# Another order of all operations for pooled attention with a SoLU layer on one core

## The chip, the cores and the metric

The kernel runs on one core of a Trainium2 chip. Time is the device time of one execution in microseconds (us); of each kernel the median of several executions is given. The engines are named as in the profile: PE is TensorE (matmuls; PEld its weight loads), DVE is VectorE, ACT is ScalarE, POOL is GpSimd, SP is SyncE, from whose queue every transfer and DMA transpose is issued.

## The reference

Attention over 8 batches and 8 heads with 576 queries and head size 64. Keys and values are averaged over 8 neighbouring rows, so 72 of each are left. The result, 4608 tokens of 512 features, goes through a layer of 1024 hidden features with SoLU (h times its own softmax), a layer norm and a second matrix:

```python
k_p = k.reshape(B, H, Sp, pool, D).mean(axis=3)
v_p = v.reshape(B, H, Sp, pool, D).mean(axis=3)
scores = scale * np.matmul(q, k_p.transpose(0, 1, 3, 2))
attn = np.exp(scores - np.max(scores, axis=-1, keepdims=True))
attn = attn / (np.sum(attn, axis=-1, keepdims=True) + 1e-09)
x = np.matmul(attn, v_p)            # then (B, S, H * D) -> (B * S, 512)
h = x @ w_in
e = np.exp(h - np.max(h, axis=-1, keepdims=True))
solu = h * (e / (np.sum(e, axis=-1, keepdims=True) + 1e-09))
mu = np.mean(solu, axis=-1, keepdims=True)
var = np.mean((solu - mu) ** 2, axis=-1, keepdims=True)
out = ((solu - mu) / np.sqrt(var + 1e-06) * g_ln) @ w_out
```

## The kernel before

The 4608 tokens are 36 tiles of 128. A group of 9 tiles serves two batches: four tiles of the even batch, one tile with the last 64 queries of both (tiles 4, 13, 22, 31), four of the odd batch. Every matrix product is made in float16 with a high and a low part of each operand, so the scale of each operand must be known first.

**Weights** (w_in is wi, w_out is wo; four quarters each, in 64 bits on the way in). Each quarter goes through w_load (SP), w_exp and w_sgn (ACT), w_shift and w_tail (DVE), w_bnd (PE), w_mul (POOL). When all four are there, w_rmax and w_all (DVE) and w_par (PE) give one scale (wi_scale, wo_scale). Then w_hi (ACT) writes the high part; the low part comes from w_res (PE) and w_lo (ACT), for two quarters of w_out from w_lod (DVE).

**Each batch.** load_kv brings k and v in three pieces (kr, vr), load_q brings q. The rows are pooled into kp and vp: by pool_kv on POOL, for batch 0 by pool_pe on PE and pool_ev on ACT, which copies the sums. a_max, a_par, a_all and a_unit give the scale of k and of v, q_max and q_scale that of q. k_hi, k_lo and k_T make k; v_hi, v_lo, v_x, r_hi, r_lo, v_rep and r_put make v (vb).

**Each tile.** In this order:
- q_hi (ACT), q_lo (DVE), q_T (a DMA transpose), scores (PE, 32 matmuls into sc);
- the softmax: s_max, s_sub (DVE), s_exp (ACT), e_sum, e_rec, e_mul (DVE), e_hi (ACT), e_lo (POOL), e_T (a DMA transpose);
- av (PE, 24 matmuls into xp), x_hi (ACT), x_lo (DVE);
- mm1, in three parts of 16 matmuls into hp; the last part needs x_lo (for tiles 0 and 1 the second);
- h_max and h_nb (DVE), h_exp (ACT), three z_scale and z_mul (DVE), z_cen and z_hi (ACT), two z_lo (POOL), z_var (ACT), two z_T (DMA transposes), n_u and n_f (POOL);
- mm2, in three parts of 16 matmuls into op, o_evac (ACT), o_store (SP).

Two buffers hold hp (pool ps_h), in turn: mm1 of a tile can start when z_mul of the tile two places earlier has read its buffer. There is one buffer each for sc (ps_s), xp (ps_x) and op (ps_o). Seven buffers (raw) hold what is loaded of k, v and the weights.

**What sets the order.** There are 2083 operations. Each takes its place from the table ORDER: for each name the places of its first, second, ... use. At the end all are issued in the order of their places; each engine works its own queue strictly in this order, and SP's queue too:

```python
def op(eng, dur, t, fn, *args, r=(), w=(), u=(), after=()):
    name = fn.__name__ + ("." + args[0] if args and isinstance(args[0], str) else "")
    count[name] = count.get(name, -1) + 1
    ops.append((ORDER[name][count[name]], fn, args))
```

```python
with tc.manual_schedule():
    for _, fn, args in sorted(ops, key=lambda o: o[0]):
        fn(*args)
```

The numbers dur, t, r, w, u and after are left from the search of an order and have no effect here. Waits between engines follow from the buffers that the operations read and write.

Of the kernel before, what the change touches and what calls it, by code (L numbers as in the profile page):

```python
# [25 lines left out]
        "a_all.v": (130, 252, 484, 790, 1026, 1176, 1480, 1803),
        "a_max.k": (34, 179, 434, 620, 864, 1120, 1352, 1596),
        "a_max.v": (128, 235, 481, 771, 1001, 1170, 1442, 1770),
        "a_par.k": (35, 182, 448, 651, 877, 1125, 1377, 1613),
        "a_par.v": (129, 236, 483, 786, 1025, 1171, 1479, 1802),  # L30
        "a_unit.k": (39, 57, 211, 213, 451, 455, 657, 663, 882, 890, 1129, 1155, 1390, 1437, 1615,
        1616),
# [5 lines left out]
        "e_T": (221, 239, 275, 332, 402, 425, 572, 497, 628, 712, 641, 761, 825, 873, 933, 957,
        1078, 1145, 1146, 1248, 1263, 1356, 1406, 1476, 1495, 1557, 1647, 1634, 1718, 1748, 1851,
        1887, 1908, 1996, 1942),  # L40
        "e_Tc": (181,),
        "e_Tp": (180,),
        "e_hi": (107, 108, 218, 219, 237, 222, 273, 272, 329, 330, 399, 373, 423, 422, 509, 508,
# [4 lines left out]
        "e_lo": (109, 220, 238, 274, 331, 401, 424, 571, 496, 604, 711, 640, 760, 824, 861, 932,  # L48
        956, 1064, 1144, 1139, 1222, 1261, 1339, 1405, 1475, 1436, 1529, 1633, 1603, 1691, 1746,
        1795, 1886, 1891, 1988, 1933),  # L50
        "e_mul": (97, 147, 195, 269, 317, 372, 415, 505, 452, 556, 689, 622, 753, 785, 820, 892,
        930, 1039, 1109, 1053, 1203, 1242, 1297, 1350, 1430, 1387, 1521, 1586, 1570, 1663, 1713,
        1791, 1834, 1867, 1958, 1924),
# [1496 lines left out]
```

## Time and profile before

| what | value |
|---|---|
| time, median of 3 runs (lowest, highest) | 487.48 us (487.16, 487.89) |
| span of the profiled execution, first to last instruction | 483.6 us |
| what lies around the span, by the median | 3.9 us |
| PE busy | 456.5 us, 94% |
| DVE busy | 372.2 us, 77% |
| ACT busy | 335.2 us, 69% |
| POOL busy | 304.5 us, 63% |

No time of the profiled execution itself was taken; the median of the runs is set beside its span. A share is a mean over the whole span; how it is spread over the opening, the middle and the end is read from the stretches. A wait is counted where an engine stands idle, and put down to what ended it.

### The profile page before, as it was taken

The page shows a single profiled execution, that of the slowest core. Times are in us where ns is not written, and L with a number is a line of the kernel's source. Part 1 is how long each engine was busy: PE and PEld are TensorE (multiplying, and loading weights), DVE is VectorE, ACT ScalarE, POOL GpSimd, SP SyncE. Part 2 cuts the span into 40 slices and gives each one's busy share as a digit, 9 for nine tenths or more (in the row PEclk, how much of TensorE's full clock was granted, in tenths as well). Part 3 has the DMA queues.
Part 4 walks back from the last instruction along what each step waited for, and adds up shares of the span by engine and source line. Part 5 has one row for each costly group of instructions (what it writes and reads, how often), then busy time and mean ns, then how long its engine had stood idle before and what let it go on. Part 6 is the DMA issues. An engine that isn't in the chain of part 4 may idle for free.

```text
span 483.6 us, 14740 instructions
## 1 busy us (share of the span) xinstructions
PE 456.5 (94%) x5976; PEld 287.7 (59%) x5976; DVE 372.2 (77%) x787; ACT 335.2 (69%) x557; POOL 304.5 (63%) x525
## 2 busy tenths in 40 slices
PE   1779899999999999999999999999999999999996
PEld 1655455655655556555556667666776666755553
DVE  5988999999889789878798867678878887462320
ACT  5598887677966688796677657587585697456361
POOL 3459737696697985858953597717758625643532
PEclk9989999999999999999999999999999999999999
DMA  8999389998999899999994999689899576861742
GB/s 309 395 354 225 86 114 219 196 193 138 213 237 213 209 173 207 204 229 229 161 215 111 215 245 172 126 136 243 167 229 190 115 137 117 138 142 24 153 108 69
DMA packets 197749, 88.92 MB, mean 184 GB/s; under 512 B 174121, under 2 KB 182321, under 8 KB 197169
## 3 DMA queue, kind: packets, MB, share of 16 engines
q1 hardware_dynamic: 197680, 87.98, 85.9%
q8 instruction: 47, 0.77, 0.6%
q14 instruction: 22, 0.17, 0.1%
HBM read 36.70 MB, written 9.44 MB: 95 GB/s over the span
## 4 chain that ended last, share of the span: by engine, by line
PE 78%; DVE 16%; DMA 2%; issue 2%; ACT 1%; SPq 0%; POOL 0%; ACTq 0%; DVEq 0%
PE op L274 35%; PE hp L274 31%; PE xp L999 4%; PE sc L274 3%; DMA kr<-in_k_dram 2%; DVE q L866 2%; DVE m L1041 1%; PE krps L410 1%; DVE sc L934 1%; DVE mx L920 1%; DVE sc L923 1%; DVE z L1073 1%; DVE e L949 1%; PE vrps L410 1%; PE res_wi L810 1%
## 5 line engine op out<-in xcount | busy, mean ns | idle before, releaser
L274 PE MATMUL hp<-wi,xT 128*64 128x512 f16 x1728 | 197.2, 379 | 2.8 <-DVE z L1073 1.4
L274 PE MATMUL op<-wo,zT 128*64 128x512 f16 x1728 | 197.2, 379 | 0.1
L274 PEld LDWEIGHTS <-xT 128*64 128x64 f16 x1728 | 106.6, 110 | 75.2 <-ACT xT L1008 2.0
L274 PEld LDWEIGHTS <-zT 128*64 128x64 f16 x1728 | 106.5, 110 | 70.6 <-DMA zT<-z 0.5
L1093 POOL TENSOR_TENSOR z<-z,z 128x512 f16<-128x512 f32 x71 | 82.0, 1167 | 67.9 <-ACT z L1087 66.4
L978 POOL TENSOR_TENSOR e<-e,e 128x512 f16<-128x512 f32 x36 | 42.2, 1173 | 39.7 <-ACT e L972 39.6
L1041 DVE TENSOR_REDUCE m<-hp 128x1 f32<-128x1024 f32 x36 | 43.8, 1217 | 23.1 <-PE hp L274 22.9
L1082 ACT ACTIVATE z<-z,sz 128x1024 f32<-128x1024 f32 x36 | 41.2, 1143 | 17.4 <-DVE z L1073 17.4
L1073 DVE SCALAR_TENSOR_TENSOR z<-hp,rs,z 128x1024 f32<-128x1024 f32 x36 | 46.1, 1280 | 9.1 <-ACT z L1052 7.9
L1052 ACT ACTIVATE z<-hp,nb,Hb 128x1024 f32<-128x1024 f32 x32 | 38.3, 1196 | 11.7 <-DVE nb L1044 9.1
L1151 ACT ACTIVATE osb<-op,f 128x512 f32<-128x512 f32 x36 | 24.5, 679 | 31.3 <-PE op L274 8.1
L1087 ACT ACTIVATE z<-z 128x1024 f16<-128x1024 f32 x36 | 37.7, 1050 | 0.9 <-DMA zT<-z 0.4
L1106 ACT ACTIVATE junk<-z 128x1024 f16<-128x1024 f32 x36 | 37.7, 1048 | 0.3
L400 POOL TENSOR_TENSOR vr<-vr 128x512 f32<-128x512 f32 (+3 forms) x42 | 36.9, 888 | 0.6
L400 POOL TENSOR_TENSOR kr<-kr 128x512 f32<-128x512 f32 (+3 forms) x42 | 36.7, 882 | 1.0 <-DMA kr<-in_k_dram 0.2
L920 DVE TENSOR_REDUCE mx<-sc 128x8 f32<-128x576 f32 x36 | 27.0, 750 | 12.9 <-PE sc L274 12.6
L934 DVE TENSOR_REDUCE sc<-sc 128x8 f32<-128x576 f32 x36 | 27.3, 759 | 12.2 <-ACT sc L930 12.1
L999 PEld LDWEIGHTS <-vb 128*64 128x64 f16 x960 | 28.9, 111 | 6.7 <-DVE vb L574 1.0
L1012 DVE SCALAR_TENSOR_TENSOR xT<-xp,xT 128x512 f16<-128x512 f32 x36 | 24.5, 681 | 8.9 <-ACT xT L1008 8.8
L999 PE MATMUL xp<-eT,vb 128*64 128x128 f16 (+1 forms) x960 | 31.0, 215 | 0.3 <-ACT e L975 0.3
L274 PEld LDWEIGHTS <-qT 128*64 128x64 f16 x1152 | 24.7, 114 | 9.9 <-ACT dg_wi L803 3.4
L1008 ACT ACTIVATE xT<-xp 128x512 f16<-128x512 f32 x36 | 21.2, 589 | 12.2 <-PE xp L999 12.2
(237 smaller groups left out, 621.3 us busy)
## 6 DMA issues: line engine op xcount, KB each, us to landing
kr<-in_k_dram SPq DMA_DIRECT2D x16, 512.0 KB
qr<-in_q_dram SPq DMA_DIRECT2D x16, 512.0 KB
vr<-in_v_dram SPq DMA_DIRECT2D x16, 512.0 KB
out_dram<-osb SPq DMA_DIRECT2D x32, 256.0 KB
wor<-in_moe_w_out_dram SPq DMA_DIRECT2D x4, 1024.0 KB
wo<-in_moe_w_in_dram SPq DMA_DIRECT2D x2, 1024.0 KB
wir<-in_moe_w_in_dram SPq DMA_DIRECT2D x2, 1024.0 KB
zT<-z SPq DMA_TRANSPOSE x72
```

What stands on the lines that cost most here:

```text
L274: nc.tensor.matmul(out[lo : lo + 64] if m > 64 else out, lhsT=lhsT[:, lo : lo + 64], **kw)
L400: nc.gpsimd.tensor_tensor(out=dst, in0=src[:, :, :n], in1=src[:, :, n : 2 * n], op=ALU.add)
L934: nc.vector.tensor_reduce(out=tl[i]["r0"], in_=s_view(i), axis=AX.X, op=ALU.add)
L978: nc.gpsimd.tensor_tensor(out=e_main(i, 1), in0=e_src(i)[0], in1=e_main(i, 0), op=ALU.subtract)
L999: nc.tensor.matmul(xp[64 * e : 64 * e + 64, c, lo:hi], lhsT=vb[b % 2][:, n, c, e], rhs=eT[:, 2 * c + e if n < 2 else H + e, lo:hi], start= ...
L1041: nc.vector.tensor_reduce(out=small(i, "m"), in_=tl[i]["hp"], axis=AX.XY, op=ALU.max)
L1052: nc.scalar.activation(z, t["hp"], AF.Exp, bias=t["nb"], scale=hsc(i, 0), accum_out=small(i, "se"))
L1073: nc.vector.scalar_tensor_tensor(out=t["z"], in0=t["hp"], scalar=t["rs"], in1=t["z"], op0=ALU.mult, op1=ALU.mult, accum_out=small(i, "sz"),)
L1082: nc.scalar.activation(t["zf"], t["zf"], AF.Identity, bias=t["sz"], scale=-float(DFF))
L1087: nc.scalar.activation(t["z16"][:, 0], t["zf"], AF.Copy)
L1093: eng.tensor_tensor(out=t["z16"][:, 1, fs], in0=t["zf"][:, fs], in1=t["z16"][:, 0, fs], op=ALU.subtract)
L1106: nc.scalar.activation(junk, t["zf"], AF.Square, scale=DFF**-0.5, accum_out=small(i, "V"))
```

## The change

The table ORDER holds other numbers; the code below it is the same, five lines further down, since the table has become five lines longer. All 2083 operations remain, with the same operands and buffers. 1395 of the 2083 places hold another operation than before, the last of them place 1856. Two lines of the table as an example:

```diff
-        "a_all.k": (36, 188, 449, 652, 881, 1126, 1380, 1614),
+    "a_all.k": (69, 188, 504, 686, 930, 1130, 1377, 1614),
```

The transfers at the start, in the order of SP's queue: before, w_in 0 and 1, k 2, w_in 2, k 1, k 0, q 0, q 1, w_in 3, w_out 0, g, w_out 1 and 2, v 2, v 1, w_out 3, v 0. Now, w_in 0, g, k 2, v 2, w_in 1 and 2, q 0, k 1, q 1, w_in 3, k 0, w_out 0 and 1, v 1, w_out 2, v 0, w_out 3 (the number is that of the quarter or piece).

PE's order of the tiles in mm1 begins 0, 1, 2, 3, 4, 5, 6, 7, 8, 9, 11, 10 before, and 0, 1, 2, 3, 4, 5, 6, 8, 7, 9, 11, 10 now.

ACT at the start, from the second quarter of w_in on. sg and u are what w_sgn and w_exp write, q_0 is q16 of tile 0, kp_0 the pooled k of batch 0 out of krps. Before:

```order
L675 ACTIVATE sg_wi1_153<-wo_86 128x1024
L634 ACTIVATE u_wi1_155<-wo_86 128x1024
L634 ACTIVATE u_wi2_171<-wir2_169 128x1024
L675 ACTIVATE sg_wi2_174<-wir2_169 128x1024
L421 ACTIVATE kp_0_87<-krps0_160 128x128
L421 ACTIVATE kp_0_87<-krps0_160 64x64
L421 ACTIVATE kp_0_87<-krps0_160 128x128
L862 ACTIVATE q16_0_218<-qr0_182,sq('b', 0)_206 128x8x64
```

Now:

```order
L639 ACTIVATE u_wi1_177<-wo_86 128x1024
L639 ACTIVATE u_wi2_179<-wir2_155 128x1024
L680 ACTIVATE sg_wi1_182<-wo_86 128x1024
L680 ACTIVATE sg_wi2_188<-wir2_155 128x1024
L867 ACTIVATE q16_0_198<-qr0_167,sq('b', 0)_194 128x8x64
L639 ACTIVATE u_wi3_205<-wir3_171 128x1024
L867 ACTIVATE q16_3_254<-qr0_167,sq('b', 0)_194 128x8x64
L867 ACTIVATE q16_1_266<-qr0_167,sq('b', 0)_194 128x8x64
L897 ACTIVATE qT0_268<-qTp0_245 128x1024
L680 ACTIVATE sg_wi3_273<-wir3_171 128x1024
L426 ACTIVATE kp_0_87<-krps0_212 128x128 x2
L426 ACTIVATE kp_0_87<-krps0_212 64x64
```

The copies into kp_0 (pool_ev) stood ahead of q_hi of tile 0 and of w_exp of the last quarter; now they stand behind three q_hi, that w_exp, the copy of qT0 and a w_sgn.

DVE ahead of z_mul of tile 4, the last row. The number in a name is the tile (mx7, sc7, r7, e7: softmax of tile 7; z4, pz4, rs4: tile 4; xT5: x_lo of tile 5) or the batch (kr2, pk2, pv2, sv2). Before:

```order
L923 TENSOR_TENSOR sc7_1820<-sc7_1820,mx7_1853 128x2x288
L492 TENSOR_REDUCE pv2_1899<-gv2_1896 128x1
L934 TENSOR_REDUCE sc7_1820<-sc7_1820 128x2x4
L940 TENSOR_SCALAR sc7_1820<-sc7_1820 128x2x4
L277 TENSOR_SCALAR pv2_1899<-pv2_1899 128x1
L1064 RECIPROCAL pz4_1752<-pz4_1752 128x1
L944 RECIPROCAL r7_1943<-sc7_1820 128x8
L499 RECIPROCAL sv2_1900<-pv2_1899 128x1
L949 TENSOR_TENSOR e7_1948<-sc7_1820,r7_1943 128x576
L1066 TENSOR_SCALAR rs4_1980<-pz4_1752,Hm0_1606 128x1
L561 TENSOR_SCALAR ct('b', 2)_1982<-pq('b', 2)_1660,pk2_1714 128x1
L1073 SCALAR_TENSOR_TENSOR z4_1742,sz4_1984<-hp4_1517,rs4_1980,z4_1742 128x1024
```

Now, the last row but three being z_mul of tile 4:

```order
L1017 SCALAR_TENSOR_TENSOR xT5_1765<-xp5_1706,xT5_1765 128x512
L1071 TENSOR_SCALAR rs4_1841<-pz4_1816,Hm0_1809 128x1
L954 TENSOR_TENSOR e8_1848<-sc8_1671,r8_1834 128x576
L871 SCALAR_TENSOR_TENSOR q16_9_1843<-qr2_1383,sq('b', 2)_1825,q16_9_1843 128x8x64
L435 TENSOR_REDUCE amx_k_95<-kp_0_87 128x1
L1078 SCALAR_TENSOR_TENSOR z4_1829,sz4_1854<-hp4_1620,rs4_1841,z4_1829 128x1024
L1017 SCALAR_TENSOR_TENSOR xT6_1887<-xp6_1862,xT6_1887 128x512
L1046 TENSOR_REDUCE m5_1923<-hp5_1769 128x1
L1049 TENSOR_SCALAR nb5_1925<-m5_1923,Hb1_1137 128x1
```

The softmax of tile 7 and the scale of batch 2's v stood ahead of z_mul of tile 4. They now stand behind it, with x_lo of tile 6 and h_max of tile 5 ahead of them.

DVE ahead of the z_mul that frees hp for mm1 of tile 9. Before, this is z_mul of tile 7, the last row (m7, nb7, pz7, rs7: its maximum and scales; sc10, sc11: softmax of tiles 10 and 11):

```order
L1041 TENSOR_REDUCE m7_2462<-hp7_2374 128x1
L430 TENSOR_REDUCE amx_k_95<-kp_1_88 128x1
L1044 TENSOR_SCALAR nb7_2465<-m7_2462,Hb1_999 128x1
L949 TENSOR_TENSOR e11_2467<-sc11_2248,r11_2460 128x576
L1059 TENSOR_SCALAR pz7_2472<-nb7_2465 128x1
L1064 RECIPROCAL pz7_2472<-pz7_2472 128x1
L578 SCALAR_TENSOR_TENSOR vb_0_91<-vp_0_89,sv2_1900,vb_0_91 64x4x64
L1066 TENSOR_SCALAR rs7_2540<-pz7_2472,Hb1_999 128x1
L920 TENSOR_REDUCE mx10_2575<-sc10_2542 128x8
L923 TENSOR_TENSOR sc10_2542<-sc10_2542,mx10_2575 128x2x288
L1073 SCALAR_TENSOR_TENSOR z7_2469,sz7_2578<-hp7_2374,rs7_2540,z7_2469 128x1024
```

Now it is z_mul of tile 8, the last row (z7 is z_mul of tile 7, amx_q the maximum of batch 3's q, sc12 the softmax of tile 12, xT9 x_lo of tile 9):

```order
L954 TENSOR_TENSOR e11_2522<-sc11_2375,r11_2520 128x576
L472 TENSOR_SCALAR pq('m', 1)_2510<-pq('m', 1)_2510 128x1
L477 RECIPROCAL sq('m', 1)_2511<-pq('m', 1)_2510 128x1
L1078 SCALAR_TENSOR_TENSOR z7_2526,sz7_2530<-hp7_2354,rs7_2517,z7_2526 128x1024
L447 TENSOR_REDUCE amx_q_97<-qr3_2291 128x1
L925 TENSOR_REDUCE mx12_2676<-sc12_2641 128x8
L1071 TENSOR_SCALAR rs8_2678<-pz8_2507,Hb1_1137 128x1
L928 TENSOR_TENSOR sc12_2641<-sc12_2641,mx12_2676 128x2x288
L1017 SCALAR_TENSOR_TENSOR xT9_2674<-xp9_2616,xT9_2674 128x512
L435 TENSOR_REDUCE amx_k_95<-kp_1_88 128x1
L1078 SCALAR_TENSOR_TENSOR z8_2605,sz8_2753<-hp8_2211,rs8_2678,z8_2605 128x1024
```

z_mul of tile 8 now comes seven rows after z_mul of tile 7, with a q_max, half a softmax, x_lo of tile 9 and a maximum of k in between.

## Rows read from the trace of the kernel before

**Rows 1.** Page, part 1: busy us, share, instructions of each engine

```profile
PE 456.5 (94%) x5976; PEld 287.7 (59%) x5976; DVE 372.2 (77%) x787; ACT 335.2 (69%) x557; POOL 304.5 (63%) x525
```

**Rows 2.** Stretches: us, busy us per engine (instructions), granted clock, DMA share, GB/s

```profile
0.00:20.00 20.00, 7.68 (x52) 7.33 (x54) 13.98 (x30) 9.17 (x13) 8.67 (x17) 1.00 0.92 339
20.00:60.00 40.00, 32.38 (x390) 19.93 (x390) 35.75 (x75) 36.56 (x58) 26.45 (x29) 0.96 0.85 242
26.00:32.00 6.00, 4.33 (x46) 2.39 (x46) 4.47 (x10) 6.00 (x8) 4.56 (x3) 0.72 1.02 395
60.00:117.00 57.00, 54.00 (x800) 32.79 (x799) 55.37 (x118) 41.87 (x73) 38.27 (x65) 1.00 0.92 174
117.00:458.00 341.00, 340.87 (x4548) 216.52 (x4543) 263.12 (x558) 238.75 (x403) 222.80 (x394) 1.00 0.89 176
458.00:484.00 26.00, 21.62 (x202) 11.11 (x196) 3.93 (x8) 8.86 (x13) 8.27 (x24) 1.00 0.37 92
```

**Rows 3.** PE's waits: waiting line, awaited line, us in total, times, longest

```profile
PE hp L274 <- DVE z L1073: 1.4, 2, 1.0
```

**Rows 4.** The chain that ended last, in order of time: start, us, what

```profile
115.89 1.22 DVE z L1073 x2
117.15 5.37 PE hp L274 x48
122.52 1.72 PE op L274 x16
...
127.96 0.67 PE xp L999 x24
...
479.80 0.69 ACT osb L1151
```

**Rows 5.** PE in order of time: start, us, tile, count, idle before and releaser

```profile
27.67 1.17 PE L274 MATMUL sc<-kT,qT 128*64 128x72 f16 x32 [3.19 <-DVE kT L536]
...
58.15 1.92 PE L274 MATMUL hp<-wi,xT 128*64 128x512 f16 x16 [0.17 <-ACT xT L1008]
...
68.03 0.69 PE L274 MATMUL sc<-kT,qT 128*64 128x72 f16 x32
68.55 7.08 PE L274 MATMUL hp<-wi,xT 128*64 128x512 f16 x64
...
81.49 3.64 PE L274 MATMUL hp<-wi,xT 128*64 128x512 f16 x32 [0.97 <-DVE z L1073]
...
92.41 3.64 PE L274 MATMUL hp<-wi,xT 128*64 128x512 f16 x32 [0.40 <-DVE z L1073]
```

**Rows 6.** DVE's lines: count, busy us, mean ns of one, idle before

```profile
L1073 DVE SCALAR_TENSOR_TENSOR z<-hp,rs,z 128x1024 f32<-128x1024 f32 x36 | 46.1, 1280 | 9.1 <-ACT z L1052 7.9
L1041 DVE TENSOR_REDUCE m<-hp 128x1 f32<-128x1024 f32 x36 | 43.8, 1217 | 23.1 <-PE hp L274 22.9
```

**Rows 7.** DVE in order of time, h_max of tile 0 and z_mul of tile 4

```profile
64.64 1.22 DVE L1041 TENSOR_REDUCE m<-hp 128x1 f32<-128x1024 f32 x1
...
115.81 1.28 DVE L1073 SCALAR_TENSOR_TENSOR z<-hp,rs,z 128x1024 f32<-128x1024 f32 x1
```

**Rows 8.** ACT in order of time: pool_ev, w_exp of w_in 3, x_hi of tile 0

```profile
18.78 0.54 ACT L421 ACTIVATE kp<-krps 128x128 f32<-128x128 f32 x3 [4.90 <-PE krps L410]
...
19.97 1.15 ACT L634 ACTIVATE u_wi<-wir 128x1024 f32<-128x1024 f32 x1
...
57.49 0.60 ACT L1008 ACTIVATE xT<-xp 128x512 f16<-128x512 f32 x1 [0.66 <-PE xp L999]
```

**Rows 9.** SP in order of time: the first transpose, us from start to issued

```profile
22.97 7.54 SPq L874 DMA_TRANSPOSE qT<-q  x1
```

**Rows 10.** Line 866 (q_lo), batches 0 and 2: ns min/median/max, first and last start

```profile
L866 DVE SCALAR_TENSOR_TENSOR q<-qr,sq('b', 0)_206,q x4: 742/749/2174, 20.4 to 46.6; 128x512 f16<-128x512 f32 x4
...
L866 DVE SCALAR_TENSOR_TENSOR q<-qr,sq('b', 2)_1661,q x4: 741/932/1676, 107.1 to 125.0; 128x512 f16<-128x512 f32 x4
```

**Rows 11.** POOL in order of time, beside the longest q_lo

```profile
46.95 2.43 POOL L400 TENSOR_TENSOR vr<-vr 128x512 f32<-128x512 f32 x2
```

**Rows 12.** Page, part 6: transfers, count, size of one

```profile
kr<-in_k_dram SPq DMA_DIRECT2D x16, 512.0 KB
qr<-in_q_dram SPq DMA_DIRECT2D x16, 512.0 KB
...
wir<-in_moe_w_in_dram SPq DMA_DIRECT2D x2, 1024.0 KB
```

More of the change, by code (lines that the diff above doesn't have):

```diff
@@ L24 @@
 ORDER = {
-        "a_all.k": (36, 188, 449, 652, 881, 1126, 1380, 1614),
[L26 to L31, printed above, removed]
@@ L40 @@
[L40 to L43, printed above, removed]
[4 rows of a table removed]
[L48 to L51, printed above, removed]
@@ new lines @@
+    "k_T": (222, 516, 729, 1015, 1153, 1494, 1669),
+    "k_Tp": (76,),
+    "k_hi": (78, 212, 510, 696, 934, 1133, 1471, 1652),
+    "k_lo": (79, 221, 515, 702, 966, 1151, 1487, 1665),
+    "load_g": (3,),
+    "load_kv": (16, 11, 4, 40, 38, 5, 153, 140, 104, 183, 204, 141, 307, 305, 306, 440, 371,
+        387, 541, 542, 543, 599, 622, 736, 793, 758, 747, 882, 901, 900, 1005, 1017, 1004,
+        1073, 1048, 1069, 1310, 1316, 1290, 1336, 1335, 1339, 1554, 1533, 1536, 1650, 1635,
+        1599),
@@ new lines @@
+    "q_lo": (33, 56, 131, 57, 220, 252, 324, 335, 381, 469, 615, 539, 513, 697, 739, 760,
+        769, 841, 1026, 953, 1074, 997, 1150, 1268, 1326, 1285, 1420, 1454, 1462, 1520,
+        1574, 1688, 1769, 1783, 1874, 1735),
+    "q_max": (27, 28, 199, 237, 157, 393, 436, 634, 653, 709, 910, 929, 1084, 1202, 1208,
+        1380, 1444, 1662, 1676, 1722),
+    "q_scale": (29, 30, 31, 202, 205, 214, 238, 243, 244, 453, 454, 455, 635, 644, 646, 711,
+        714, 722, 935, 936, 947, 1111, 1116, 1141, 1221, 1234, 1235, 1446, 1447, 1448, 1675,
+        1677, 1678, 1723, 1725, 1727),
@@ new lines @@
+    "v_hi": (149, 130, 368, 343, 572, 571, 836, 837, 1089, 1090, 1256, 1267, 1507, 1522,
+        1808, 1809),
+    "v_lo": (185, 142, 380, 374, 582, 578, 857, 861, 1149, 1122, 1277, 1303, 1508, 1578,
+        1818, 1823),
+    "v_rep": (165, 352, 623, 868, 1158, 1287, 1498, 1846),
+    "v_x": (187, 174, 373, 379, 583, 577, 855, 846, 1092, 1135, 1284, 1293, 1625, 1540,
+        1828, 1821),
+    "w_all.wi": (63,),
+    "w_all.wo": (133,),
+    "w_bnd.wi": (8, 43, 44, 48),
+    "w_bnd.wo": (90, 116, 117, 118),
@@ new lines @@
+    "w_dg.wi": (86,),
+    "w_dg.wo": (195, 150),
+    "w_exp.wi": (1, 17, 18, 36),
+    "w_exp.wo": (74, 85, 94, 106),
+    "w_hi.wi": (92, 109, 91, 110),
+    "w_hi.wo": (167, 159, 248, 291),
+    "w_lo.wi": (152, 146, 113, 164),
+    "w_lo.wo": (229, 210),
+    "w_load": (0, 6, 7, 13, 34, 35, 39, 59),
+    "w_lod.wo": (312, 311, 300, 309),
+    "w_mul.wi": (15, 22, 26, 55),
+    "w_mul.wo": (84, 114, 228, 262),
+    "w_par.wi": (62,),
+    "w_par.wo": (132,),
+    "w_pwi": (108,),
+    "w_pwo": (194,),
@@ new lines @@
+    "w_res.wi": (151, 127, 112, 158),
+    "w_res.wo": (196, 180),
+    "w_rmax.wi": (52,),
+    "w_rmax.wo": (120,),
+    "w_sgn.wi": (14, 20, 25, 53),
+    "w_sgn.wo": (75, 97, 227, 261),
+    "w_shift.wi": (2, 19, 23, 37),
+    "w_shift.wo": (77, 87, 98, 107),
+    "w_tail.wi": (9, 21, 24, 51),
+    "w_tail.wo": (83, 105, 99, 189),
+    "wi_scale": (73,),
+    "wo_scale": (135,),
+    "x_hi": (211, 242, 271, 326, 390, 434, 477, 586, 530, 669, 788, 726, 839, 874, 944, 983,
+        1030, 1099, 1172, 1200, 1258, 1332, 1397, 1434, 1513, 1547, 1629, 1702, 1658, 1757,
+        1788, 1853, 1921, 1950, 1999, 1976),
```

248 lines of the change are left out of this document (102 added, 146 removed), and 90 rows, old and new, of the table ORDER.

## The prediction

> **What bounds the kernel now.** I read the engines' busy time first, then that by stretches, TensorE's waits, the chain, and at last the instructions at the places that these point to. PE is busy for 456.5 us of the span of 483.6 us [rows 1], so 27.1 us are to be had at most. The stretches say where they lie [rows 2]: PE idles 12.3 us before 20 us, 7.6 us from 20 to 60, 3.0 us from 60 to 117, 0.1 us from 117 to 458, and the rest behind the last matmul, which the last evacuation and store fill. PE's only repeated wait for DVE on the way there is that of mm1 for z_mul [rows 3]. So the end is the moment from which PE runs without a gap, plus the work it then still has, plus a tail of 3.8 us from 479.80 on [rows 4]. Only the first 117 us can change the time.
>
> In them PE waits for DVE. DVE is busy for 55.37 of the 57 us from 60 to 117 [rows 2], and the chain in this stretch is one DVE instruction after another until z_mul of tile 4, after which mm1 of tile 6 starts at 117.15 [rows 4]. The mechanism is the pair of hp buffers: mm1 of a tile needs the buffer that z_mul of the tile two places earlier frees. Its signs are the same wait of 0.97 us at 81.49 and of 0.40 us at 92.41 [rows 5]. From 117.15 on DVE keeps ahead.
>
> **The change part by part.** It adds and removes nothing: each engine has the same operations, so PE's work, the tail and the sums of all engines stay. It moves operations in the queues, and what counts is how much DVE work stands ahead of an hp hand-over, and how much PE work. I count both from one point of the trace: DVE done with z_mul of tile 4 at 117.0, PE at mm1 of tile 6 at 117.15 [rows 4]. Where the new order has less DVE work ahead of a hand-over, DVE gets there earlier; where PE has less work ahead, PE is there earlier too; the difference is the gain that this place allows, and the smallest decides.
>
> Prices. PE: 1.73 us for each third of mm1 or mm2 (16 matmuls), 0.67 for av [rows 4], 0.52 for scores (68.03 to 68.55) [rows 5]. DVE: the mean durations by line, as 1.28 for z_mul and 1.22 for h_max [rows 6], from the same view for the others. In a full queue they overlap: from h_max of tile 0 at 64.64 to z_mul of tile 4 at 115.81 [rows 7] the single durations add up to 54.2 us, and 51.2 us passed. So I take 0.94 of a sum.
>
> Place 1, mm1 of tile 6. Fifteen DVE operations no longer stand ahead of z_mul of tile 4: the softmax of tile 7, the scale and k_lo of batch 2's k, and the maximum and scale of its v. Durations 6.2 us, times 0.94 is 5.8: DVE is done at 111.2. PE loses scores of tile 9 and one a_par ahead of it (0.58), so it would stand there at 116.6. Allowed: 5.3 us.
>
> Place 2, last third of mm1 of tile 4, which needs x_lo of that tile. Against z_mul of tile 4, DVE has 19.9 us less ahead, times 0.94 is 18.7: 98.3. PE has 4 thirds of mm1, 3 of mm2, 2 av, 3 scores and two a_par less: 12.1 + 1.3 + 1.6 + 0.1 = 15.1, so 102.0. Allowed: 3.7 us.
>
> Place 3, mm1 of tile 9. The new order puts tile 8 before tile 7, and mm1 of tile 9 now takes the buffer of tile 8, whose z_mul comes behind z_mul of tile 7 and behind q_max of batch 3. Beyond z_mul of tile 4 DVE has 32.1 us of work up to it (63 operations, among them 4 h_max, 4 z_mul and 4 x_lo), times 0.94 is 30.2: 147.2. PE has 9 thirds of mm1, 8 of mm2, 3 av, 2 scores, a v_rep (0.25) and an a_par more: 29.4 + 2.0 + 1.0 + 0.3 = 32.7, so 149.9. Allowed: 2.6 us. The other hand-overs allow 4.3 us or more, and behind tile 9 the gap widens, as DVE has only 263 us of work for 341 us [rows 2].
>
> The opening. These sums suppose that DVE idles in it as long as before: 4.25 us from 20 to 60 [rows 2]. Two things differ. ACT no longer stands 4.90 us before the pooled k of batch 0 [rows 8], since that evacuation is now behind two steps of the weights and three of q. Against it, the last piece of k is loaded behind all of w_in, and k's scale comes only at about 26 us. I followed the new queues of ACT and DVE with the durations of the rows. The first q scale is ready at 18.9, w_in's scale at 26.7, the four w_hi of w_in at 38, e_mul of tile 0 at 39, x_hi of tile 0 at about 55, where it ended at 58.1 before [rows 8]. DVE waits 3.4 us in it: twice some 1 us for s_exp of tiles 1 and 2, for which ACT is late, and small ones; that is 0.9 us less than before. Taken at its word the walk ends 2.7 us before the count alone, but it gives ACT its closest spacing and no late signal. I take 0.9, with 0 and 2.7 as the ends.
>
> TensorE's clock. From 26 to 32 us the granted clock was 0.72 on average [rows 2], with PE idle for most of the time before; scores of tile 0 took 1.17 us there, 0.69 at the full clock [rows 5]. The new order leaves PE as thin before 20 us, so I expect a stretch at 1.2 GHz again; a longer one costs 0.5 us on the first softmax, a vanished one gives as much. I take nothing.
>
> SP's queue. Loads and transposes change places, mostly by a few ranks. Behind an early transpose that waits, the loads of batch 1 wait; their cover is that POOL's sums of batch 1 are first needed at about 50 us. Taken at nothing; uncovered, a transpose that is one 3 us issue late [rows 9] stalls a scores by that much.
>
> Sum: 2.6 (place 3) + 0.9 (opening) = 3.5 us, less than the 4.6 that place 2 then allows. The profiled span of 483.6 becomes 480.1. The median of the timed runs is 487.48, 3.9 us above the span; start and end of the program stay, so the time is 484.0 us.
>
> **The rivals.**
> (a) More is gained: the opening gives all of 2.7, and place 3 allows 5.3, place 2 6.4: 482.2 us. For it: the walk itself. Against it: DVE's waits are met at random, and each late one is lost.
> (b) The gain goes to DVE's long forms. The same q_lo took between 0.742 and 2.174 us [rows 10], the long one at 46.61 beside POOL's sums of v [rows 11]. The new order lays other POOL work beside DVE's q_lo, v_lo and w_lod. Three more long forms before place 3 cost 3 x 1.4 = 4.2 us and take the 3.5: 487.5 to 488.3. Against it: the old order has such forms too (q_lo of batch 2 at up to 1.676 [rows 10]), and they can fall out as well as in. The Trainium skill (SBUF — State Buffer, Who interferes with whom) has a rule for it: the port pair that DVE and GpSimd share is an exclusive lock, and the one that comes second is blocked for the whole instruction. By it the trace's long forms are waits, which agrees, and an order that was searched without this lock would lose part of what it found.
> (c) Slower: k of batch 0 comes too late. Its last piece now stands behind 6.0 MB of loads, where before 3.8 MB stood ahead of it (1 MB for each quarter of w_in, 0.5 MB for each large piece of q or k [rows 12]). In the old order the last piece of w_in, at the same depth, was used at 19.97 [rows 8], so I put k at about 20.4. k's sums, scale, scores and softmax of tile 0 hang on it, and with them x_lo. If it lands 6 us later, all of the opening is 6 us later and 3.5 - 6 = 2.5 us are lost: 490 us. It decides from a delay of 3.5 us on. For it: the issues stand in a full queue by then (the first transpose took 7.54 us to issue [rows 9]). Against it: the amount ahead is the same as for that piece of w_in.
> That the change does nothing is not among them: the queues differ as the rows on the change show.
>
> **How the numbers follow.** The forecast with its neighbourhood (482.3 to 486.4, gains of 1 to 5 us) has 0.60, (a) 0.10, (b) 0.17, (c) 0.13. A measurement of this kernel tells some 0.2%, 1 us, from no change. Faster by more is the forecast and (a): 0.70. Of (b) 0.14 falls within 1 us of the old time, 0.03 beyond; with (c) slower has 0.16. The range leaves out (c) and half of (a): 481.9 to 488.3.
>
> **What would show it.** In the profile after: mm1 of tile 0 starting near 55 to 56.5 us instead of 58.15; mm1 of tile 6 at about 112 to 113; PE's waits for z_mul gone at tiles 3 and 4, and one of up to a microsecond before tile 9, near 146 us; PE from there to the last matmul without idle time, and that at about 476.3; DVE over 95% busy from 60 to 140. Wrong would be: idle time of PE behind 150 us, on DMA or POOL (then the queues that I took at nothing decide), x_hi of tile 0 later than 58 (c), or an early start whose gain is lost between 60 and 117 (b).

## The result and the profile after

The new order takes 492.22 us (median of 4 runs, 490.38 to 494.23) against 487.38 us (4 runs, 487.16 to 487.89): 1.0103 times the old one, 95% interval 1.0068 to 1.0137. The forecast was 484.0 us in a range of 481.9 to 488.3, so the time lies outside it and on the other side. The profiled execution took 491.0 us with a span of 488.9 us, so 2.1 us lie around the span. For the old order the same difference is 1.7 us in the executions that were timed with the experiments (a span of 483.6 us in one of 485.29 us). The profile of before was therefore one of the old order's shortest executions, and the "3.9 us around the span" were partly the distance from it to the median.

What the new order does to PE is told from its idle time. Page, part 1, and the stretches of [rows 2] for the new order (us, busy us of each engine with the count of instructions, granted clock, DMA share, GB/s):

```profile
PE 456.9 (93%) x5976; PEld 283.0 (58%) x5976; DVE 372.2 (76%) x787; ACT 334.9 (69%) x557; POOL 309.6 (63%) x525
```

```profile
0.00:20.00 20.00, 5.48 (x40) 5.15 (x40) 14.38 (x26) 7.99 (x8) 8.01 (x17) 1.00 0.94 345
20.00:60.00 40.00, 33.58 (x372) 22.14 (x371) 35.16 (x79) 35.60 (x58) 20.25 (x22) 0.96 0.78 230
26.00:32.00 6.00, 4.68 (x85) 3.91 (x84) 4.02 (x13) 4.82 (x9) 2.29 (x1) 0.97 1.02 397
60.00:117.00 57.00, 54.70 (x812) 32.40 (x810) 53.53 (x112) 46.01 (x77) 44.09 (x67) 1.00 0.91 182
117.00:458.00 341.00, 336.16 (x4516) 209.34 (x4514) 263.90 (x563) 233.71 (x400) 227.34 (x394) 1.00 0.90 173
```

PE's work is the same (456.9 us, 456.5 in [rows 1]). Its idle time per stretch is 14.5, 6.4, 2.3 and 4.8 us, where [rows 2] give 12.3, 7.6, 3.0 and 0.1: 2.2 us more at the start, 1.9 less from 20 to 117, and 4.7 more behind 117. That is 5.0 of the 5.3 us between the spans. The largest part stands in the stretch that the prediction held to be safe.

PE's waits in the new order (waiting line, awaited line, us in total, times, longest):

```profile
...
PE krps L415 <- DMA kr<-in_k_dram: 6.7, 1, 6.7
PE sc L279 <- DVE e L954: 3.4, 2, 2.7
PE op L279 <- DMA zT<-z: 2.0, 3, 1.1
PE qTp L888 <- DVE q L871: 1.8, 1, 1.8
...
PE xp L1004 <- DVE pk L497: 1.2, 1, 1.2
PE op L279 <- ACT osb L1156: 1.1, 1, 1.1
PE xp L1004 <- DMA eT<-e: 0.7, 2, 0.5
...
```

The wait of mm1 for z_mul [rows 3] is gone. In its place stand waits for DMA transposes (zT, eT), for an evacuation that waits for a store (osb), and for DVE behind a late load of q. One view says more than the list, two long stretches of the old order, and then of the new one. The column before the last is the mean busy share of the 16 DMA engines:

```profile
0.00:100.00 100.00, 77.33 (x992) 50.28 (x992) 89.05 (x185) 75.20 (x118) 59.34 (x82) 0.98 0.90 238
100.00:300.00 200.00, 199.60 (x2766) 122.66 (x2766) 170.13 (x365) 145.41 (x249) 150.01 (x262) 1.00 0.99 197
```

```profile
0.00:100.00 100.00, 78.42 (x985) 50.70 (x987) 87.86 (x184) 75.55 (x117) 58.92 (x82) 0.98 0.83 231
100.00:300.00 200.00, 193.75 (x2662) 121.74 (x2660) 167.69 (x359) 142.40 (x248) 147.70 (x252) 1.00 1.00 195
```

From 100 to 300 us the DMA engines are as full as PE by this measure, in the old order too (0.99). It adds up the times of packets and can pass 1 (1.03 in old_opening, 1.05 in before_extra, both below), so 0.99 alone does not show that nothing more fits in. By 100 us the DMA engines of the new order were busy for 0.07 x 100 = 7 us less. Most of that is made good soon: by 117 us it is 3 us, and the transfers have moved as much as in the old order (26.5 and 26.4 MB, GB/s times length of the stretches up to there).

Where the time is lost shows at two places that have the same operations of PE ahead of them in both orders. These are mm1 of tile 11 and scores of tile 24, in the old order, then in the new one:

```profile
158.18 2.11 PE L274 MATMUL hp<-wi,xT 128*64 128x512 f16 x18
298.41 0.72 PE L274 MATMUL sc<-kT,qT 128*64 128x72 f16 x32
```

```profile
157.95 1.89 PE L279 MATMUL hp<-wi,xT 128*64 128x512 f16 x16
303.72 0.71 PE L279 MATMUL sc<-kT,qT 128*64 128x72 f16 x32 [0.24 <-DMA qT<-q]
```

At 158 us the new order is level with the old one; at scores of tile 24 it is 5.3 us late, and it stays so to the end. The whole loss falls between the two.

### The profile page after: what moved, and what is told of

It reads as the page before. It is cut to its first block, busy times and chain, and to the rows that moved or that the text cites. A ratio compares the mean times of both kernels' runs of the same rounds, so it can differ in the third digit from the quotient of the medians.

```text
span 488.9 us, 14699 instructions
## 1 busy us (share of the span) xinstructions
PE 456.9 (93%) x5976; PEld 283.0 (58%) x5976; DVE 372.2 (76%) x787; ACT 334.9 (69%) x557; POOL 309.6 (63%) x525
## 4 chain that ended last, share of the span: by engine, by line
PE 53%; DMA 6%; ACT 4%; DVE 3%; POOL 3%; SPq 3%; issue 1%; ACTq 0%; POOLq 0%; DVEq 0%
PE op L279 26%; PE hp L279 22%; PE xp L1004 3%; PE sc L279 2%; DMA kr<-in_k_dram 1%; DMA qT<-q 1%; DMA out_dram<-osb 1%; DMA qr<-in_q_dram 1%; DMA zT<-z 1%; POOL e L983 1%; SPq L993 1%; ACT z L1057 1%; DMA vr<-in_v_dram 1%; ACT osb L1156 1%; DVE z L1078 1%
## 5 line engine op out<-in xcount | busy, mean ns | idle before, releaser
L279 PEld LDWEIGHTS <-zT 128*64 128x64 f16 x1728 | 103.8, 110 | 76.9 <-DMA zT<-z 2.8
L279 PEld LDWEIGHTS <-xT 128*64 128x64 f16 x1728 | 104.0, 110 | 75.3 <-ACT xT L1013 2.1
L1013 ACT ACTIVATE xT<-xp 128x512 f16<-128x512 f32 x36 | 21.2, 590 | 14.8 <-PE xp L1004 14.7
L977 ACT ACTIVATE e<-e 128x512 f16<-128x512 f32 x36 | 22.2, 620 | 13.0 <-DVE e L954 9.3
```

What stands on the lines that cost most here:

```text
L279: nc.tensor.matmul(out[lo : lo + 64] if m > 64 else out, lhsT=lhsT[:, lo : lo + 64], **kw)
```

## Experiments

All ratios are to the old order on the same chip, which took 486.65 to 487.15 us beside the experiments. The table gives PE's idle time between its operations in the profile of each kernel, up to av of tile 0 (the opening), from there to 130 us, and behind 130 us, and PE's busy time, which grows where the granted clock is low. A profile is one execution: that of hole_and_late was the longest of ten (491.43 us), that of opening_new the shortest of six (494.33). late_new and mid_loads have no idle times here, since their profiled executions (498.45 and 497.33 us) were far above their medians.

| kernel | us | ratio, 95% interval | opening | to 130 | behind | PE busy |
|---|---|---|---|---|---|---|
| old order | 487.38 | | 19.8 | 3.2 | 0.1 | 456.5 |
| new order | 492.22 | 1.0068 to 1.0137 | 20.9 | 2.5 | 4.7 | 456.9 |
| opening_new | 497.3 | 1.0182 to 1.0241 | 21.0 | 8.7 | 0.9 | 458.0 |
| late_new | 491.93 | 1.0068 to 1.0124 | | | | |
| early_new | 496.26 | 1.0161 to 1.0219 | 21.8 | 2.4 | 4.9 | 460.9 |
| middle_new | 492.6 | 1.0091 to 1.0139 | 20.1 | 3.1 | 4.4 | 459.6 |
| old_opening | 489.99 | 1.0049 to 1.0102 | 20.5 | 3.7 | 2.4 | 458.1 |
| late_mended | 491.52 | 1.006 to 1.0111 | 20.6 | 1.4 | 1.9 | 461.1 |
| both_mended | 492.09 | 1.0069 to 1.0128 | 22.3 | 3.2 | 2.2 | 458.4 |
| mid_loads | 493.88 | 1.0083 to 1.0161 | | | | |
| store_late | 490.3 | 1.004 to 1.0083 | 19.5 | 3.4 | 2.6 | 457.7 |
| hole_closed | 491.17 | 1.006 to 1.0103 | 21.2 | 1.4 | 3.9 | 458.7 |
| hole_and_late | 489.65 | 1.0021 to 1.0064 | 21.2 | 1.2 | 4.7 | 458.5 |
| old_with_hole | 490.32 | 1.0039 to 1.0088 | 22.3 | 2.8 | 0.4 | 458.5 |
| old_plus | 487.42 | 0.999 to 1.002 | 20.7 | 4.1 | 0.4 | 457.1 |
| k0_early | 492.74 | 1.0068 to 1.0134 | 20.8 | 2.2 | 2.3 | 461.5 |
| after_nostore | 486.88 | 0.9989 to 1.0033 | 21.4 | 2.0 | 0.4 | 458.5 |
| before_nostore | 486.88 | 0.999 to 1.0019 | 19.9 | 3.3 | 0.1 | 457.7 |
| hole_nostore | 486.35 | 0.9962 to 0.9996 | 20.4 | 2.4 | 0.5 | 458.9 |
| before_extra | 558.95 | 1.1444 to 1.1505 | 20.3 | 6.0 | 49.0 | 480.5 |

**Parts of the order.** The two orders hold nearly the same operations up to places 221 (some 57 us) and 632 (some 137 us), so they can be joined there. Theory A: the rows behind 137 us are misplaced. Theory B: the late loads of the opening are inherited.

```diff
-order = new
+late_new:    old[:632], then the rest as in new
+early_new:   new[:632], then the rest as in old
+opening_new: new[:221], then the rest as in old
+middle_new:  old[:221], new up to its 632nd, then the rest as in old
+old_opening: old[:221], then the rest as in new
```

late_new: 

> The old order for the first 632 operations (up to about 137 us), the new order for the rest. Theory A (the loss lies in the rows of the new order behind 137 us, where PE lost 4.4 us to late transposes, a late q load and a late store): PE still loses 3 to 5 us there, so 490.5 to 492.5 us. Theory B (the new opening issues its loads late and the later transfers inherit that): the late waits are gone, 487.0 to 488.0 us.

early_new: 

> The new order for the first 632 operations, the old order for the rest. Theory A: PE idles 23.7 us up to 137 us, where it was 22.9, and nothing behind: 487.5 to 488.5 us. Theory B: the late waits come although the rows behind 137 us are the old ones: 490.5 to 492.5 us.

opening_new: 

> The new order for the first 221 operations (the opening, up to mm1 of tile 0 at about 57 us), the old order for the rest. By the traces PE lost 20.9 us in the new opening against 19.9 in the old one. Theory A: that 1.0 us stays and the waits for z_mul between 60 and 117 us are taken up in part by it (they are waits for DVE, and DVE idled 0.6 us more in the new opening): 487.6 to 488.4 us. Theory B, with its late transfers from the opening alone: 490 us and more.

middle_new: 

> The old opening (221 operations), the new order up to the 632nd operation, then the old order. Theory A: the waits for z_mul go (1.4 us), waits for transposes of zT and eT take their place in part (the new order leaves 7 to 13 us from e_mul to av where the old one left 12 to 24): PE idle in 60 to 137 us falls from 3.0 to some 1.5 to 2.8 us, so 486.0 to 487.5 us. If the new middle were as good as the count of DVE work ahead of the hand-overs said (2.6 us), it would be 484.8 us.

late_new took 491.93 us (1.0068 to 1.0124), as theory A had it. Its opening and middle are the old ones, so theory B's late loads are not there to be inherited, and it loses as much as the whole new order. early_new took 496.26 and middle_new 492.6, as neither theory had it; opening_new took 497.3, in theory B's range. Every part of the new order costs time by itself, and all parts together cost less than the opening alone. Part of that is the joint: in early_new and middle_new PE waits 1.2 us for scores of tile 10 and 3.0 for av of tile 9, directly behind place 632. In opening_new it waits 4.4 us for the maximum of batch 1's v, whose pieces the new opening loads later than the old rows use them. So each order's loads and uses are fitted to each other, and these joints are in the times too: A is favoured by late_new, but the runs don't settle it.

**Single rows.** In the new order the store of tile 7 stands behind that of tile 12 in SP's queue. These are PE's wait and SP's stores of the new order (start, us, ..., idle before and what ended it):

```profile
245.64 1.70 PE L279 MATMUL op<-wo,zT 128*64 128x512 f16 x14 [1.13 <-ACT osb L1156]
```

```profile
239.55 0.53 SPq L1166 DMA_DIRECT2D out_dram<-osb  x1
249.03 0.67 SPq L1166 DMA_DIRECT2D out_dram<-osb  x1
257.67 0.53 SPq L1166 DMA_DIRECT2D out_dram<-osb  x1
```

They are the stores of tiles 11, 12 and 7. Tile 7 holds one of two output buffers from 211 to 258 us, so the evacuation of tile 12 has to wait until the store of tile 11 has landed, and mm2 of tile 13 for that evacuation. Moving rows in the new order, and this one row in the old one:

```diff
 late_mended (new order)
 SP:  load_q 4 0
+SP:  load_q 4 1        (was 5 DMA issues later, at 198.97 us)
 ACT: o_evac 7
+SP:  o_store 7         (was at 257.67 us)
 PE:  mm2 6 0
+PE:  mm2 6 1           (was behind scores 13)
 PE:  mm1 10 0
+PE:  a_par.v 3         (was ahead of mm1 10 0)
 mid_loads (new order)
 SP:  load_kv 2 vr 2
+SP:  load_q 2 1, load_kv 2 vr 0   (were at 100.28 and 101.92 us)
 both_mended: all six
 store_late (old order)
-SP:  o_store 7         (at 209.31 us)
 SP:  o_store 12
+SP:  o_store 7
```

late_mended: 

> The new order with four operations moved by a few places: the second load of batch 4's q to right behind the first, the store of tile 7's result to right behind its evacuation, mm2 of tile 6 (second third) ahead of scores of tile 13, a_par of batch 3's v behind the first third of mm1 of tile 10. Theory A (each late wait has its own misplaced row): the four waits of PE behind 137 us go, 0.69 + 0.52 + 1.15 + 1.13 = 3.5 us, and 492.2 becomes 488.0 to 489.5 us. Theory C (SP's queue as a whole runs behind, the rows are only where it shows): other waits take their place, 491 to 493 us.

mid_loads: 

> The new order with two loads of batch 2 (second piece of q, first of v) moved from between the transposes of tiles 2 and 6, at 100 to 102 us, to right behind the loads of v at 92 us. Theory A: the waits of PE for z_T of tile 2 (1.13 us) and e_T of tile 6 (0.52 us) go, as those transposes no longer share the DMA engines with 1 MB of loads: 490.3 to 491.0 us. Theory C: the earlier loads delay the transposes of tiles 8 and 5 instead: 492 us or more.

both_mended: 

> The new order with both sets of moves, six operations. Theory A: the gains add, 492.2 - 3.5 - 1.6 = 487.1 us (486.5 to 488.0), which is no better than the old order, because the new opening still loses 1 us more. Theory C: 490 us or more.

store_late: 

> The old order with one operation moved: the store of tile 7's result from 209 us to behind that of tile 12, at about 250 us, where the new order has it. Theory A: it holds one of two output buffers, so each evacuation waits for the store before it; PE waits 1 to 2.5 us at mm2 of tile 13 near 245 us, and less at tiles 11 and 12: 488.2 to 490 us. If the store's place does not matter: 487.0 to 487.5 us.

The one store moved makes the old order 3.6 us slower (490.3 against 486.75). Its trace shows the wait and its cause, PE first, then ACT:

```profile
236.81 1.92 PE L274 MATMUL op<-wo,zT 128*64 128x512 f16 x16 [1.88 <-ACT osb L1151]
248.45 5.37 PE L274 MATMUL op<-wo,zT 128*64 128x512 f16 x48 [0.36 <-ACT osb L1151]
```

```profile
236.07 0.69 ACT L1151 ACTIVATE osb<-op,f 128x512 f32<-128x512 f32 x1 [3.73 <-DMA out_dram<-osb]
247.71 0.69 ACT L1151 ACTIVATE osb<-op,f 128x512 f32<-128x512 f32 x1 [4.00 <-DMA out_dram<-osb]
```

So that cause is shown. In late_mended and both_mended this wait of the new order is gone, and so are those before scores of tile 13 and av of tile 14. But the time fell by 0.7 us only (491.52), where 3.5 were expected, and both_mended is no better. The idle time does not explain that by itself: in the profile of late_mended it is 4.2 us less than in that of the new order (23.9 against 28.1), and PE is busy 4.2 us longer (461.1 against 456.9), with a granted clock of 0.66 from 50 to 60 us where the new order's profile has 1.00. The same two places as above, in late_mended:

```profile
161.09 1.89 PE L274 MATMUL hp<-wi,xT 128*64 128x512 f16 x16
303.72 0.71 PE L274 MATMUL sc<-kT,qT 128*64 128x72 f16 x32 [0.47 <-DMA qT<-q]
```

PE comes to the first 3.1 us later than in the new order and to the second at the same time, and waits for a transpose there. In seven kernels with the new rows and all stores (the new order, old_opening, late_mended, both_mended, hole_closed, hole_and_late, k0_early) mm1 of tile 11 begins between 157.95 and 162.00 us and takes until 303.08 to 305.49 to reach scores of tile 24: 143 to 146 us, the longest for the earliest start, where the old order takes 140.2. So something other than PE sets the pace there. The two loads moved forward (mid_loads, 493.88 us) gave nothing either: in both_mended PE waits 2.61 us for z_T of tile 2, where the new order has 1.13. So moving single rows (theory A) was not enough, and the times are those of theory C (the transfers are late as a whole). That other waits take the place of those mended, as theory C has it, does not show in late_mended; it shows in hole_and_late (below).

**The hole in the opening.** In the new opening PE waits 2.69 us for the softmax of tile 1, directly ahead of the w_res of w_out:

```profile
51.30 0.71 PE L279 MATMUL sc<-kT,qT 128*64 128x72 f16 x32 [2.69 <-DVE e L954]
```

In the profile of the changed kernel the granted clock is 1.00 behind it. In nine of the eleven kernels with the new opening it is 0.66 or 0.83 from 50 to 60 us, in the others 1.00; three of the nine are those in which the hole was closed. In the traces of the old order, store_late, old_plus, middle_new, old_opening and before_nostore, all with the old opening and no wait over 1.1 us there, it is 1.00.

```diff
 hole_closed (new order)
 DVE: w_all.wo
+DVE: s_max 1, s_sub 1          (were behind wo_scale, r_lo, v_lo)
 DVE: wo_scale, r_lo 0
+DVE: e_sum 1, e_rec 1, e_mul 1 (were behind v_lo and q_max)
 ACT: v_hi 0
+ACT: s_exp 1                   (was behind w_dg and w_lo)
 hole_and_late: these and the four moves of late_mended
 old_with_hole (old order)
 DVE: wo_scale
+DVE: q_lo 3, r_lo 0, v_lo 0    (were behind e_mul 1)
 DVE: e_sum 1, e_rec 1, e_mul 1
 old_plus (old order)
 DVE: x_lo 0
+DVE: q_max b1, s_max 3         (were ahead of x_lo 0)
 DVE: z_mul 1
+DVE: w_lod 2 1                 (was ahead of z_mul 1)
 DVE: z_mul 2
+DVE: q_lo 7                    (was ahead of z_mul 2)
```

hole_closed: 

> The new order with the softmax of tile 1 earlier: its maximum and subtraction ahead of the scale of w_out, its exp right behind v_hi of batch 0, its sum and multiplication ahead of v_lo and q_max. In the traces with the new opening PE idles 2.7 us before scores of tile 2 (at 48.6 to 51.3 us), and in four of six of them the granted clock is 0.50 to 0.60 in the 4 to 6 us behind it, which makes av of tile 0 2.8 to 3.7 us later. Theory D (this hole is the largest loss of the new opening, and the clock falls because of it): the hole shrinks to under 0.7 us, the clock stays at 1.00 from 30 us on, 492.2 becomes 487 to 489.5 us. Theory E (the hole only moves on to av or mm1 of tile 0, and the clock falls in either case): 491 to 493 us.

hole_and_late: 

> The softmax of tile 1 earlier as in the run before, and the four late moves as well (load of q of batch 4, store of tile 7, mm2 of tile 6, a_par of batch 3's v). Theory D: the gains add, PE idles some 22 to 23 us in all as in the old order, 485 to 487.5 us. Theory E: 490 to 492 us.

old_with_hole: 

> The old order with a hole made in it: q_lo of tile 3, r_lo and one v_lo of batch 0 ahead of the sum and multiplication of the softmax of tile 1, so that scores of tile 2 start 2 to 3.5 us later with PE idle before them (0.40 us before). Theory D: the granted clock falls to about half for several us behind the hole in most executions, and w_res there takes twice its time: hole plus clock less the 0.9 us that a later wait absorbs, 489 to 492 us. If the hole does not touch the clock: 487.8 to 489 us.

old_plus: 

> The old order with five DVE operations moved behind what PE waits for: q_max of batch 1 and s_max of tile 3 behind x_lo of tile 0, one w_lod behind z_mul of tile 1, q_lo of tile 7 behind z_mul of tile 2. The waits of PE at mm1 of tiles 0, 3 and 4 (0.49, 0.97 and 0.40 us in the profile of before) go. If what counts is where PE waits for DVE: 485.0 to 486.0 us. If DVE is the bound of the whole stretch, mm1 of tile 6 waits for z_mul of tile 4 by as much instead: 486.5 to 487.2 us.

The hole made in the old order, and the stretch behind it (granted clock third from the end):

```profile
50.29 1.17 PE L274 MATMUL sc<-kT,qT 128*64 128x72 f16 x32 [3.89 <-DVE e L949]
51.39 2.08 PE L810 MATMUL res_wi<-wir,dg_wi 128*128 128x512 f32 x2
53.57 1.06 PE L810 MATMUL res_wi<-wir,dg_wi 128*128 128x512 f32 x2
```

```profile
50.00:60.00 10.00, 9.32 (x76) 5.08 (x77) 6.17 (x17) 4.62 (x7) 4.17 (x6) 0.83 0.15 50
```

Scores took 1.17 us and the first pair of w_res 2.08, where the later pair took 1.06: PE ran at 1.2 GHz behind a hole of 3.9 us. The kernel lost 3.6 us (490.32 against 486.68). That part of theory D is shown. The rest of it fell. In hole_closed the hole shrank to 0.49 us, but waits of 1.08 and 0.69 us came behind it and the clock fell as before, as theory E had it. In this kernel the clock doesn't decide the time: its five executions, at granted clocks from 0.990 to 0.999 of the span, all took 491.01 to 491.59 us. That does not hold for the new order itself, whose executions took 490.38 and 491.00 us at 0.995, 493.44 at 0.988 and 494.23 at 0.993. hole_and_late took 489.65 us, between the two expectations; its interval lies below that of the new order, so the two sets of moves together gave back more than half of the 4.8 us. In its profile, with 1.2 us of idle time from av of tile 0 to 130 us, it has 4.7 again behind, and not at the mended rows.

```profile
303.08 0.71 PE L274 MATMUL sc<-kT,qT 128*64 128x72 f16 x32 [1.42 <-DMA qT<-q]
358.53 0.86 PE L999 MATMUL xp<-eT,vb 128*64 128x128 f16 x24 [1.27 <-DMA eT<-e]
```

These are scores of tile 24 and av of tile 28, whose neighbours stand as in the old order, where PE comes 5 to 6 us earlier and doesn't wait. So in this execution PE waits for transposes behind for most of what it gained ahead. old_plus, with four operations moved, is level (487.42): its moves take the waits of mm1 for z_mul from the old order too, and others come for them, 0.88 us in mm2, 0.82 at mm1 of tile 4 and 0.91 at scores of tile 8.

**DMA work taken away and added.** Theory F has two halves: the DMA engines are the bound from 100 us on, and the new order has 7 us of their work in arrears there.

```diff
 after_nostore (new), before_nostore (old), hole_nostore (hole_closed)
 def o_store(eng, i):
     osb = tl[i]["osb"]
+    if i < 18:
+        tl[i] = None
+        return
 k0_early (new order)
 SP:  load_kv 0 kr 1
+SP:  load_kv 0 kr 0            (was behind load_q 0 1 and w_load wi 3)
+PE:  pool_pe 0 kr 0            (was behind w_bnd of wi 3)
 PE:  q_Tp 0
 before_extra (old order), in o_store
+    if i < 18:
+        last = out[(B - 1) * S : (B - 1) * S + SA, :].rearrange("(p s) n -> s p n", s=4)
+        eng.dma_start(
+            last[i % 4].rearrange("(h a) n -> h a n", h=2),
+            v[i % 8, 0:2, :512].rearrange("h (a j) d -> h a (j d)", j=8),
+        )
```

after_nostore: 

> The new order with the stores of the results of tiles 0 to 17 left out (4.7 MB of DMA, some 15 us of all DMA engines up to about 300 us), so half of the output is not written. Theory F (the DMA engines are almost a second bound: they are 1.00 busy from 100 to 300 us, and the new order leaves them idle in the opening, 8.3 times 10 us of work done by 100 us against 9.0, so that PE catches up with transfers that are late as a whole): the waits behind 137 us (4.4 us) go nearly all, 487 to 488.8 us. Theory A (single misplaced rows): only the wait for the store of tile 11 goes (1.1 us), 490.5 to 491.5 us.

before_nostore: 

> The old order with the same stores left out. PE idles 0.1 us behind 117 us there, so both theories expect little: 485.8 to 487.0 us. By theory F it is then within 2 us of the new order without these stores; by theory A 4 us or more below it.

old_opening: 

> The old order for the first 221 operations (opening, up to 57 us), the new order for the rest: the counterpart of the run that had the new opening alone. Theory F: the DMA work is ahead as in the old order when the new rows begin, so the waits behind 137 us shrink to under 2 us, 487 to 489 us. Theory A: they stay, and with the new waits at transposes in the middle 490.5 to 493 us.

k0_early: 

> The new order with the last piece of batch 0's k loaded right behind its second piece, ahead of q's second piece and of w_in 3, and its sums on PE ahead of the transpose of tile 0's q. Its buffer is then free at some 24 instead of 27 us, for which the load of w_out 3 and, behind it, the first transpose and the loads of batch 1 wait, and PE's hole of 1.76 us before that transpose is filled. Theory F: the DMA engines idle less between 24 and 40 us and the late waits shrink: 488.5 to 490.5 us. If the opening's DMA does not matter: 490 to 491.5 us for the hole alone.

before_extra: 

> The old order with DMA work added: ahead of each of the first 18 stores a transfer of 0.25 MB from v to rows of the output that the last stores write again, 4.7 MB in all, some 15 us of all DMA engines between 95 and 290 us. No engine waits for these transfers themselves. Theory F (the old order stands just within what the DMA engines can do there): PE gets waits behind 117 us where it has none, and the time rises by 3 to 10 us, 490 to 497 us. If there is slack: under 1 us, 486.5 to 487.7 us.

hole_nostore: 

> The new order with the softmax of tile 1 earlier (which gave 1.05 us, 491.17 against 492.22) and without the stores of tiles 0 to 17. Theory F: with the DMA engines relieved the earlier PE is no longer given back, and the same move gives about the 1.7 us of idle time that it took away: 484.5 to 486.0 us against 486.88. If the move is worth the same in either case: 485.8 us; if the clock of TensorE decides: no better than 486.9 us.

Without half of the stores the new order takes 486.88 us, the old one 486.88 as well, both on one chip. So all of the 4.8 us between the two orders (492.22 against 487.38) are gone, and the old order gains nothing (1.0004, 0.999 to 1.0019). These are the two long stretches of after_nostore, and the waits of its PE between 100 and 458 us:

```profile
0.00:100.00 100.00, 77.77 (x954) 52.22 (x956) 85.66 (x176) 72.86 (x114) 56.63 (x80) 0.95 0.81 224
100.00:300.00 200.00, 198.50 (x2714) 128.18 (x2712) 173.59 (x371) 146.26 (x251) 153.35 (x257) 1.00 0.93 180
```

```profile
PE xp L1004 <- DMA eT<-e: 1.2, 2, 0.9
PE vr L279 <- DVE xT L1017: 0.3, 1, 0.3
```

The DMA share falls to 0.93, PE's idle time behind 130 us from 4.7 to 0.4 us, and all waits behind 139 us are gone, also those for q and for the softmax that no store had to do with. From mm1 of tile 11 to scores of tile 24 PE takes 140.5 us, nearly the 140.2 of the old order. That is what the first half of theory F says and theory A denies (1.1 us). What lies ahead of 100 us stays as bad as it was, 0.81 and 21.4 us of idle time, so the second half is not needed: the loss goes although no more is done by 100 us.

old_opening (489.99 us) gave half of the late waits back, 2.4 us of 4.7, with a DMA share of 0.87 up to 100 us, between 0.90 and 0.83, and a time between the two expectations. But the share up to 100 us does not decide how much PE waits later: it is 0.85 in old_plus and 0.83 in old_with_hole, which have 0.4 us of idle time behind 130. There PE was busy for 76.1 and 75.4 us by 100 us, 78.4 in the new order, so it was itself later. k0_early missed: 492.74 us where 488.5 to 490.5 was expected. The hole before q_Tp went, but that before scores of tile 2 stayed (2.49 us), the clock was low behind it, and the DMA engines idled no less. before_extra went the way that theory F has it, by far too much: 558.95 us instead of 490 to 497, with 49 us of idle time behind 130 us, on qT and eT above all, and PE busy for 24 us longer, at a granted clock of 0.91 from 100 to 300 us. These transfers slow the transposes themselves (below), so the run shows that the old order can't take them, and not how much DMA time it has to spare. hole_nostore: 486.35 against 486.88 is not told apart from no gain; that the opening's gain would count in full without the DMA bound is therefore not shown.

No order that ran beats the old one with all of its output written.

What stays open: a store takes time in SP's queue as well as on the DMA engines, so the runs put the loss on the transfers, and not on the one rather than the other. SP is not idle either: from 100 to 300 us the issues in its queue add up to 157 us in the new order, 151 in the old one and 138 in after_nostore. Which rows behind 137 us make the new order need more of either is known for the four mended ones alone.

## Why the prediction was wrong

**What bounds the kernel.** This is the step that failed: "Only the first 117 us can change the time". It rested on PE's 0.1 us of idle time from 117 to 458 us in [rows 2]. That PE doesn't wait there shows that the transfers come just in time, not that they have time to spare. The same row gives a DMA share of 0.89, a mean in which 100 to 300 us stand at 0.99. With it, "SP's queue ... Taken at nothing" was the term of the sum that was mis-sized: it was priced as single late issues, and it measured 4.7 us, PE's idle time behind 130 us, which falls to 0.4 when half of the stores are left out.

**Places 1 and 2.** The count of DVE work came near: z_mul of tile 4 was put at an end of 111.2 us and ended at 112.7, where it had been 117.1, and no mm1 waits for z_mul. At place 2 PE did gain: the last third of mm1 of tile 4 began at 99.1 us, where the count had PE at 102.0 without a gain. But mm1 of tile 6 began at 115.7, not at 112 to 113, and mm1 of tile 9 at 149.86, where it had 149.9 without a gain. PE lost its time to the opening and to waits for transposes (1.13 us at mm2 of tile 2, 0.52 at av of tile 6), which the new order leaves less room: from e_mul to av of tiles 6 to 11 lie 8 to 11 us, where the old order had 15 to 24. The count asked only when DVE hands over hp, not when the results of the same DVE work have come through ACT, POOL, SP's queue and a transpose.

**Place 3** was misread, and the section on the change has it wrong too: mm1 of tile 9 does not take the buffer of tile 8. DVE's two z_mul of tiles 7 and 8, and PE:

```profile
144.79 1.27 DVE L1078 SCALAR_TENSOR_TENSOR z<-hp,rs,z 128x1024 f32<-128x1024 f32 x1
149.56 1.27 DVE L1078 SCALAR_TENSOR_TENSOR z<-hp,rs,z 128x1024 f32<-128x1024 f32 x1
```

```profile
149.86 3.40 PE L279 MATMUL hp<-wi,xT 128*64 128x512 f16 x30
```

mm1 of tile 9 starts while z_mul of tile 8 still reads its buffer: it took that of tile 7, free since 146.1 us. The forecast wait near 146 us did not come, and the bound of 2.6 us was none.

**The opening** was to give 0.9 us and cost 1.1 (PE idles 20.9 us up to av of tile 0, 19.8 before). The walk ran too early at each mark: q's first scale was put at 18.9 us and came at 20.8, w_in's at 26.7 and came at 29.8, x_hi of tile 0 at about 55 and ended at 57.8. mm1 of tile 0 began at 58.22 us, not at 55 to 56.5. The first miss has one row, on DVE, and POOL beside it:

```profile
14.91 3.03 DVE L662 SCALAR_TENSOR_TENSOR wir<-wir,u_wi 128x1024 int32<-128x1024 int32 x1
```

```profile
14.40 2.45 POOL L683 TENSOR_TENSOR wo<-wo,sg_wi 128x1024 f32<-128x1024 f32 x1 [3.08 <-DVE wo L662]
```

This w_tail took 3.03 us where the one before it took 1.23, and it ended 1.1 us behind the end of the w_mul that had started first. In opening_new, late_mended, hole_closed, k0_early and after_nostore it took 3.03 to 3.04 us too. It is rival (b) in one place, and the trace agrees with the rule of the Trainium skill that the prediction names there (SBUF — State Buffer, Who interferes with whom), by which the second one is blocked for the whole instruction of the first: 16.85 + 1.23 = 18.08, and it ended at 17.94. As the course of the whole, (b) was not it: the sixteen q_lo of the first four batches took 0.73 to 0.75 us each, and z_mul was on time.

**Rival (c)** did not come: the last piece of k was there when PE came to it, at 23.7 us. What is slower by 5 us has a cause that none of the rivals named, and the chance of 0.16 for slower was in (c) for the greater part.

**TensorE's clock.** The stretch at 1.2 GHz before 30 us came as expected (granted clock 0.50 from 24 to 26 us). The one between 50 and 60 us, in nine of the eleven kernels with this opening though not in the profile of the new order itself, was not foreseen, nor was the hole at 48.6 to 51.3 us: the walk added up DVE's waits of about 1 us for s_exp and did not ask how long PE would stand in one piece.
